# A spectral filter and a gated MLP on one core: the forward token transform in fp32 instead of three fp16 products

## The chip, the core and the metric

The kernel runs on one core of a Trainium2 chip. A core has a matrix engine (TensorE, PE in the profile; its weight loads are PEld), VectorE (DVE), ScalarE (ACT), GpSimd (POOL) and SyncE (SP), which here issues the DMAs. Each engine executes its own list of instructions in order and waits at semaphores for the others. SBUF holds operands; PE writes its sums to PSUM, from which ACT and DVE read them. The metric is the device time of one execution in microseconds (us), lower is better.

## The reference

The input `x` is 2048 tokens by 448 features, fp32. It is normalized over the features, and the normalized `xn` goes two ways:

```python
X = rfft2(xn)                       # over tokens and features
A = irfft2(X * (w_r + 1j * w_i))    # a filter in the frequency domain
gate = xn @ W_gate                  # 448 -> 1792
up   = xn @ W_up
h = gate * (gate > 0) * up
B = h @ W_down                      # 1792 -> 448
return x + A + B
```

## The kernel before

Both ways run at once. The matrix products of the MLP (gate and up, called `gu`, and down, `dn`) are the steady stream of PE. The Fourier transforms are cut into many small steps, mostly on DVE, that are strewn between them as background.

Precision is kept by splitting: a fp32 number is held as a high and a low fp16 half, and a product is three fp16 matmuls, high by high, high by low and low by high. Weights are split as they arrive (ACT makes the high half, DVE the low one, L924 and L928; for the down weights L957 and L961), and so is the activation `h` (L1028 to L1040: Relu on ACT, times up on DVE, high half on ACT, low half on DVE).

The two-dimensional transform is built in stages. The 2048 tokens are 16 residues by 128. The feature transform (`f_dft`, fp16 halves, 48 small matmuls of 58 columns) is done for two residues `a` and `a + 8` at a time. `f_fold` (L515) reads its PSUM and makes `Fq[a]`, the tile `eo` of the profile, fp32, of which there are two buffers. `f_a` and `f_b` (L444 to L467) take an eight-point transform over feature groups in place, on DVE. Then comes the token transform over 64 points, `f_sdft`, which this change touches. `f_hi` (ACT, L531) and `f_lo` (DVE, L534) split `eo` into the two fp16 halves `Xh`, for each of the two residues. `f_sdft` multiplies them by the table `fm`, in the four 64x64 quadrants of the array: quadrant (k, b) takes the rows of half k and writes the columns of half b. Its three products times four quadrants are 12 matmuls of 464 columns, and there are eight `f_sdft`, for a = 0, 4, 2, 6, 1, 5, 3, 7. Its result lies in the PSUM tile `fx`, of which there is one buffer of two banks, and `f_y1` reads it: ACT copies residue a to SBUF (L591), and DVE forms sum and difference with residue a + 8 (L596, L597). Further butterflies over the residues (`join2`, `join3`, L568 to L584), the filter product (L665 to L671), the inverse stages, the inverse token transform (`i_sdft`, `fx<-im,vt`) and the inverse feature transform (`i_ddft`, `fx<-idc_t,wf`) follow. The inverse stages need the butterflies of all sixteen residues.

The order of the work is set in three ways. The opening, to about 45 us, is written out by hand. After it the program walks through the MLP units, and hands out background items between them by credit: each item has a cost on DVE in microseconds (the number in `add`), and a factor `load` is found so that the costs of all items fill the room beside the units up to a place near the end. Then a list scheduler places the instructions on each engine by dependences and priorities. So a change to the items or their costs moves the background against the MLP everywhere after the opening. Gate and up sums use two PSUM tiles (`gu`) in turn: PE can start a unit only when DVE has read the one before the last (L1032).

Of the kernel before, what the change touches and what calls it, by code (L numbers as in the profile page):

```python
# [9 lines left out]
F16 = mybir.dt.float16  # L10
# [12 lines left out]
XW = NG * GW  # L23
# [77 lines left out]
def _constants():  # L101
# [17 lines left out]

    n1 = np.arange(64)  # L120
    k1, sine = _k1()
    c_fm = np.zeros((8, 2, 64, 2, 2, 64), np.float16)
    c_im = np.zeros((8, 128, 2, 2, 64), np.float16)
    for n2 in range(16):
        th = 2 * np.pi * (np.outer(16 * n1 + n2, k1) % S) / S
        w = np.where(sine[None, :], np.sin(th), np.cos(th))
        w[:, ROW] = (-1.0) ** n1
        c_fm[n2 % 8, n2 // 8] = np.stack(_split(w * sc), axis=1).reshape(64, 2, 2, 64).transpose(0, 2, 1, 3)
        c_im[n2 % 8, :, n2 // 8] = np.stack(_split(w.T * sc), axis=1)


# [18 lines left out]
    for s in range(8):  # L150
        th = 2 * np.pi * (np.outer(kp, m + s) % D) / D
        o = slice(56 * (s // 2), 56 * (s // 2) + 56)
        for c, t in enumerate((g * np.cos(th) * 8 / 7, -g * np.sin(th) * 8 / 7)):
            p = 64 * (s % 2) + 32 * c
            c_id[p:p + KC, :, o] = np.stack(_split(t), axis=1)
    c_fm = c_fm.reshape(2, 4, 128, 2, 2, 64).transpose(1, 2, 0, 3, 4, 5)
# [6 lines left out]
def tile_gfnet_reglu(ctx: ExitStack, tc: tile.TileContext, x, xr, wgu, wd, wf, ident, c_fd, c_fm, c_im, c_row, c_id,  # L163
# [70 lines left out]
    def ft(shape, dt, name, bufs=1):  # L234
        return fwd_pool.tile(shape, dt, name=name, bufs=bufs)
# [40 lines left out]
        nc.sync.dma_start(wdst[f], wdv[f])  # L276

    def load_fm(q):
        t = ft([128, 2, 2, 2, 64], F16, "fm", 4)
        nc.sync.dma_start(t, c_fm[q])  # L280
        for j in range(2):
            fm_t[q + 4 * j] = t[:, j]
# [253 lines left out]
    def f_sdft(a):  # L536
        m, w, ps = None, fm_t[a], fx2()
        for k in range(2):
            yps[a + 8 * k] = ps[:, k, 0:XW].rearrange("p (g c k) -> p g c k", g=NG, c=2)
        for i, (x, y) in enumerate(((0, 0), (0, 1), (1, 0))):  # L540
            for k in range(2):
                for b in range(2):
                    p, q = slice(64 * k, 64 * k + 64), slice(64 * b, 64 * b + 64)
                    xh = Xh[a + 8 * b].rearrange("p a g k -> p a (g k)")
                    with tc.high_priority(offset=0 if m is None else 2000):
                        m = chained(mm(ps[q, k, 0:XW], w[p, b, x], xh[p, y], start=(i == 0), stop=(i == 2),
                                       skip_group_check=True).ins, m)
        return m

    def rotate(t, b, p, sgn):  # L550
# [601 lines left out]
    for k, a in enumerate(seq):  # L1152
        gap = k and extra.get(k - 1)
        for second in (False, True):
            if second:
                add(1.99, f_a, a)
            if k and second != bool(gap):
                for n2 in (seq[k - 1], seq[k - 1] + 8):
                    add(1.09 * (n2 >= 8), f_y1, n2)
            if k < 7 and second != bool(gap):  # L1160
                add(0.0, offer, f_dft, seq[k + 1], seq[k + 1] + 8)
        add(2.14, f_b, a)
        for n2 in (a, a + 8):
            add(0.0, f_hi, a, n2)
        if k < 7:
            add(0.0, force, f_dft, seq[k + 1], seq[k + 1] + 8)
            add(1.27, f_fold, seq[k + 1])
        for n2 in (a, a + 8):
            add(0.54, f_lo, a, n2)
        add(0.0, f_sdft, a)  # L1170
        for fn, q in extra.get(k, ()):
            fn(q)
# [379 lines left out]
```

## Time and profile before

| | |
|---|---|
| time, median of 3 runs (lowest to highest) | 454.19 us (453.86 to 454.76) |
| the profiled execution: its time, its span | 452.46 us, 450.7 us |
| PE busy | 427.8 us, 95% of the span |
| DVE busy | 394.4 us, 88% |
| ACT busy | 252.8 us, 56% |
| mean granted PE clock | 0.985 |

The span goes from the first to the last instruction of the profiled execution. The page gives for each group of instructions its line, engine, operation, tiles (output<-inputs), count, busy time and mean duration, and behind the bar the idle time of the engine just before them with what ended it. Successive instructions of an engine overlap, so that the distance from start to start is less than the duration: a matmul of 512 columns lasts 380 ns by its group's mean, and twelve of `gu` take 2.70 us in the chain of waits. The page in forty slices:

```profile
PE   6999999999999999999999999979999973999997
DVE  6898898997987998999999999999998989958513
```

### The profile page before, as it was taken

The numbers are of one execution on the slowest core, as the hardware profiler recorded it, in microseconds if no ns is written. First come the engines' busy times: TensorE is split into PE (matmuls) and PEld (weight loads), VectorE is DVE, ScalarE is ACT, GpSimd is POOL, SyncE is SP. The second block draws the span as 40 slices with busy tenths as digits, with TensorE's granted clock in tenths as the row PEclk, the third lists the DMA queues.
The fourth block names the chain that finished last, engine by engine and source line by source line (L and its number), as shares of the span: only waits on it lengthen the run. The fifth ranks groups of instructions, "written<-read, shape, count | busy, mean of one in ns | idle before, by whom it ended". The sixth has DMA issues, their size and how long they took to land.

```text
span 450.7 us, 8697 instructions
## 1 busy us (share of the span) xinstructions
PE 427.8 (95%) x3254; PEld 203.4 (45%) x3254; DVE 394.4 (88%) x952; ACT 252.8 (56%) x508; POOL 32.2 (7%) x72
## 2 busy tenths in 40 slices
PE   6999999999999999999999999979999973999997
PEld 2644544444444444444444444434545432444544
DVE  6898898997987998999999999999998989958513
ACT  6897392387359746615434553935675663563630
POOL 1140030031001401000000010010000000000000
PEclk9999999999999999999999999999999995999999
DMA  8769948015002235334330310022122112300212
GB/s 263 243 165 291 373 118 123 2 36 72 3 2 93 67 117 155 81 89 123 87 84 1 100 27 1 1 55 53 29 50 70 37 35 51 105 22 1 83 42 81
DMA packets 37722, 38.63 MB, mean 86 GB/s; under 512 B 18928, under 2 KB 33072, under 8 KB 37680
## 3 DMA queue, kind: packets, MB, share of 16 engines
q1 hardware_dynamic: 37680, 38.09, 30.8%
q8 instruction: 25, 0.41, 0.4%
q14 instruction: 17, 0.14, 0.1%
HBM read 23.20 MB, written 3.67 MB: 60 GB/s over the span
## 4 chain that ended last, share of the span: by engine, by line
PE 51%; DVE 38%; ACT 6%; issue 2%; DMA 2%; SPq 0%; DVEq 0%; ACTq 0%
PE gu L476 31%; PE dn L476 13%; PE fx L476 4%; DVE h L1040 3%; DVE g L1032 3%; DVE y L568 2%; DVE y L569 2%; DVE wt L928 2%; ACT junk L219 2%; DVE y L665 2%; DVE y L668 2%; DVE y L583 2%; DVE y L706 1%; DVE y L584 1%; DVE y L707 1%
## 5 line engine op out<-in xcount | busy, mean ns | idle before, releaser
L476 PE MATMUL gu<-T,wt 128*128 128x512 f16 (+2 forms) x1250 | 270.9, 377 | 4.5 <-DVE g L1032 4.5
L476 PEld LDWEIGHTS <-wt 128*128 128x128 f16 (+1 forms) x1250 | 111.4, 98 | 148.3 <-issue 29.1
L476 PE MATMUL dn<-wdt,h 128*128 128x448 f16 x624 | 127.5, 353 | 0.0
L476 PEld LDWEIGHTS <-h 128*128 128x128 f16 x624 | 60.2, 98 | 57.9 <-issue 0.8
L1036 ACT ACTIVATE h<-g 128x512 f16<-128x512 f32 x56 | 35.1, 627 | 76.7 <-DVE g L1032 76.6
L1032 DVE SCALAR_TENSOR_TENSOR g<-gu,g 128x512 f32<-128x512 f32 x56 | 38.2, 683 | 14.3 <-ACT g L1028 14.2
L1040 DVE TENSOR_TENSOR h<-g,h 128x512 f16<-128x512 f32 x56 | 38.3, 685 | 10.0 <-ACT h L1036 9.9
L1028 ACT ACTIVATE g<-gu 128x512 f32<-128x512 f32 x56 | 32.8, 585 | 17.7 <-PE gu L476 17.7
L1068 ACT ACTIVATE xy<-dn,dsc 128x448 f32<-128x448 f32 x44 | 27.3, 624 | 12.8 <-PE dn L476 12.8
L1057 ACT ACTIVATE dn<-xy,dinv 128x448 f32<-128x448 f32 x44 | 27.5, 631 | 0.5
L928 DVE SCALAR_TENSOR_TENSOR wt<-wst,wsc,wt 128x512 f16<-128x512 f32 x28 | 20.3, 742 | 2.6 <-ACT wt L924 2.6
L222 POOL PARTITION_ALL_REDUCE wm<-wm x15 | 9.0, 598 | 161.0 <-ACT junk L219 161.0
L924 ACT ACTIVATE wt<-wst,wsc 128x512 f16<-128x512 f32 x28 | 19.1, 713 | 1.8 <-DVE wsc L229 1.8
L219 ACT ACTIVATE junk<-wst 128x512 bf16<-128x512 f32 x28 | 17.4, 620 | 1.3 <-DMA wst<-in_wgu 1.1
L810 ACT ACTIVATE vt<-wst,fsc 128x928 f16<-128x928 f32 x8 | 8.8, 1099 | 10.8 <-DVE wst L467 10.8
L957 ACT ACTIVATE wdt<-wdst,wds 128x448 f16<-128x448 f32 x14 | 8.7, 658 | 8.5 <-DVE wds L953 8.5
L569 DVE TENSOR_TENSOR y<-y,y 128x464 f32<-128x464 f32 x21 | 13.3, 633 | 0.1
L568 DVE TENSOR_TENSOR y<-y,y 128x464 f32<-128x464 f32 x21 | 13.3, 632 | 0.1
L657 ACT ACTIVATE wf<-wf 128x116 f32<-128x116 f32 x16 | 4.5, 293 | 15.8 <-DMA wf<-in_wf 15.8
L839 DVE SCALAR_TENSOR_TENSOR yu<-fx,yu 128x512 f32<-128x512 f32 x16 | 11.0, 687 | 2.6 <-ACT yu L834 2.3
L860 ACT ACTIVATE fx<-xy,fsc 128x448 f32<-128x448 f32 x14 | 8.8, 629 | 7.9 <-DVE yu L839 7.9
L291 DVE BATCH_NORM_STATS2 bst<-y 128x6 f32<-128x448 f32 x16 | 9.2, 617 | 4.3 <-DMA y<-in_xr 4.3
(164 smaller groups left out, 506.2 us busy)
## 6 DMA issues: line engine op xcount, KB each, us to landing
wst<-in_wgu SPq DMA_DIRECT2D x28, 256.0 KB, 4.7
wf<-in_wf SPq DMA_DIRECT2D x16, 232.0 KB, 2.8
sw<-y SPq DMA_DIRECT2D x64, 58.0 KB, 2.0
sw<-wst SPq DMA_DIRECT2D x32, 116.0 KB, 2.2
y<-in_xr SPq DMA_DIRECT2D x16, 224.0 KB, 4.9
xy<-in_x SPq DMA_DIRECT2D x16, 224.0 KB, 5.0
out<-xy SPq DMA_DIRECT2D x15, 224.0 KB, 1.9
wdst<-in_wd SPq DMA_DIRECT2D x14, 224.0 KB, 4.6
```

Source lines behind the costliest of these rows:

```text
L219: A.activation(mt([128, 512], BF16, "junk")[:, 0:src.shape[-1]], src, AF.Square, scale=SQ, accum_out=acc)
L476: r = P.matmul(*a, **k)
L568: V.tensor_tensor(t, a, b, op=OP.add)
L569: V.tensor_tensor(d, a, b, op=OP.subtract)
L924: A.activation(w[:, 0:4, :], wst[f, g], AF.Copy, scale=wsc[f, g])
L928: V.scalar_tensor_tensor(w[:, 4:8, :], st, sc, w[:, 0:4, :], op0=OP.mult, op1=OP.subtract)
L1028: last["A"] = A.activation(g1s[f, q], hps[f, q][:, 0, :], AF.Relu, scale=2.0 ** -22).ins
L1032: last["V"] = V.scalar_tensor_tensor(g1, hps[f, q][:, 1, :], 2.0 ** -22, g1, op0=OP.mult, op1=OP.mult).ins
L1036: A.activation(ht[f, q][:, 0, :], g1s[f, q], AF.Copy)
L1040: V.tensor_tensor(h[:, 1, :], g1s.pop((f, q)), h[:, 0, :], op=OP.subtract)
L1057: A.activation(dps[n2][:, 0:D], xy[n2], AF.Copy, scale=dinv[:, g:g + 1])
L1068: last["A"] = A.activation(xy[n2], dps[n2][:, 0:D], AF.Copy, scale=dsc[:, g:g + 1]).ins
```

## The change

The split before the token transform is left out. `f_hi` and `f_lo` are no longer called, and `f_sdft` multiplies the fp32 part of `Fq[a]` (`f_part`, a strided view of `eo`) by an fp32 table, one matmul for each quadrant instead of three. The table holds the unsplit numbers, at the same size in bytes. The items of `f_hi` and `f_lo`, the latter at 0.54 us each, leave the list of the background, by which `load` and all that follows is set. The functions `f_hi` and `f_lo` stay in the text but are not used.

```diff
-    c_fm = np.zeros((8, 2, 64, 2, 2, 64), np.float16)
+    c_fm = np.zeros((8, 2, 64, 2, 64), np.float32)
...
-        c_fm[n2 % 8, n2 // 8] = np.stack(_split(w * sc), axis=1).reshape(64, 2, 2, 64).transpose(0, 2, 1, 3)
+        c_fm[n2 % 8, n2 // 8] = (w * sc).reshape(64, 2, 64)
...
     def load_fm(q):
-        t = ft([128, 2, 2, 2, 64], F16, "fm", 4)
+        t = ft([128, 2, 2, 64], F32, "fm", 4)
...
     def f_sdft(a):
         m, w, ps = None, fm_t[a], fx2()
...
-        for i, (x, y) in enumerate(((0, 0), (0, 1), (1, 0))):
-            for k in range(2):
-                for b in range(2):
-                    p, q = slice(64 * k, 64 * k + 64), slice(64 * b, 64 * b + 64)
-                    xh = Xh[a + 8 * b].rearrange("p a g k -> p a (g k)")
-                    with tc.high_priority(offset=0 if m is None else 2000):
-                        m = chained(mm(ps[q, k, 0:XW], w[p, b, x], xh[p, y], start=(i == 0), stop=(i == 2),
-                                       skip_group_check=True).ins, m)
+        for k in range(2):
+            for b in range(2):
+                p, q = slice(64 * k, 64 * k + 64), slice(64 * b, 64 * b + 64)
+                with tc.high_priority(offset=0 if m is None else 2000):
+                    m = chained(mm(ps[q, k, 0:XW], w[p, b], f_part(a, a + 8 * b)[p], start=True, stop=True,
+                                   skip_group_check=True).ins, m)
...
         add(2.14, f_b, a)
-        for n2 in (a, a + 8):
-            add(0.0, f_hi, a, n2)
         if k < 7:
             add(0.0, force, f_dft, seq[k + 1], seq[k + 1] + 8)
             add(1.27, f_fold, seq[k + 1])
-        for n2 in (a, a + 8):
-            add(0.54, f_lo, a, n2)
         add(0.0, f_sdft, a)
```

Line numbers behind the touched functions are smaller by 2 in the changed kernel (L596 becomes L594, L1032 becomes L1030), and by 6 at its end.

How instructions stand on PE at the seventh token transform, before (buffer numbers kept; the two `Xh` are the two residues):

```order
L476 MATMUL dn_2383<-wdt_604,h_2158 128x448
L476 LDWEIGHTS fm_1301
L476 MATMUL fx_2006<-Xh_1946,fm_1301 64x464
L476 LDWEIGHTS fm_1301
L476 MATMUL fx_2006<-Xh_1948,fm_1301 64x464
```

and now:

```order
L476 LDWEIGHTS h_1794
L476 MATMUL dn_2327<-wdt_601,h_1794 128x448
L476 MATMUL fx_1898<-eo_1775,fm_1269 64x464 x4
L476 LDWEIGHTS h_1794
L476 MATMUL dn_2327<-wdt_601,h_1794 128x448
```

Twelve pairs of a weight load and a matmul have become four matmuls without a weight load between them, on the fp32 tiles.

On DVE, the end of the forward part, before. L466 and L467 end the last eight-point transform, L596 and L597 are the butterflies that read a token transform's PSUM (the second pair those of the last one), L1032 and L1040 the gate product and the low half of `h`:

```order
L467 SCALAR_TENSOR_TENSOR eo<-bw 128x2x116
L961 SCALAR_TENSOR_TENSOR wdt<-wdst,wds,wdt 128x448
L596 TENSOR_TENSOR y_81<-y_73,fx 128x464
L597 TENSOR_TENSOR y_69<-y_73,fx 128x464
L1032 SCALAR_TENSOR_TENSOR g_2335<-gu,g_2335 128x512
L534 TENSOR_TENSOR Xh<-eo,Xh 128x464 x2
L1040 TENSOR_TENSOR h<-g_2335,h 128x512
L1032 SCALAR_TENSOR_TENSOR g_2377<-gu,g_2377 128x512
L1040 TENSOR_TENSOR h<-g_2377,h 128x512
L596 TENSOR_TENSOR y_78<-y_75,fx 128x464
L597 TENSOR_TENSOR y_77<-y_75,fx 128x464
```

and now:

```order
L467 SCALAR_TENSOR_TENSOR eo<-bw 128x2x116
L951 TENSOR_SCALAR wds<-wds 128x5
L959 SCALAR_TENSOR_TENSOR wdt<-wdst,wds,wdt 128x448 x2
L1030 SCALAR_TENSOR_TENSOR g_2266<-gu,g_2266 128x512
L1038 TENSOR_TENSOR h<-g_2266,h 128x512
L594 TENSOR_TENSOR y_78<-y_75,fx 128x464
L595 TENSOR_TENSOR y_77<-y_75,fx 128x464
L566 TENSOR_TENSOR y_73<-y_81,y_78 128x464
L567 TENSOR_TENSOR y_75<-y_81,y_78 128x464
L1030 SCALAR_TENSOR_TENSOR g_2321<-gu,g_2321 128x512
```

The two subtractions of the split are gone, one gate product stands behind the last butterflies of the forward part instead of ahead of them, and the butterflies of the seventh transform have moved further ahead.

The gate product that follows next on DVE, before:

```order
L583 SCALAR_TENSOR_TENSOR y_69<-y_79,y_67 128x464
L584 SCALAR_TENSOR_TENSOR y_75<-y_79,y_67 128x464
L961 SCALAR_TENSOR_TENSOR wdt<-wdst,wds,wdt 128x448
L568 TENSOR_TENSOR y_67<-y_72,y_78 128x464
L569 TENSOR_TENSOR y_79<-y_72,y_78 128x464
L1032 SCALAR_TENSOR_TENSOR g_2592<-gu,g_2592 128x512
L575 TENSOR_TENSOR y_72<-y_82,y_77 128x8x29
```

and now:

```order
L581 SCALAR_TENSOR_TENSOR y_69<-y_79,y_67 128x464
L582 SCALAR_TENSOR_TENSOR y_75<-y_79,y_67 128x464
L1030 SCALAR_TENSOR_TENSOR g_2502<-gu,g_2502 128x512
L566 TENSOR_TENSOR y_67<-y_72,y_78 128x464
L567 TENSOR_TENSOR y_79<-y_72,y_78 128x464
L731 SCALAR_TENSOR_TENSOR rowh<-row,rowh 16x232
```

The product stands ahead of the butterfly (L568 and L569, now L566 and L567) that preceded it. Two weight splits further up and the one shown (L961, now L959) stand behind it as well.

More of the change, by code (lines that the diff above doesn't have):

```diff
@@ L155, in _constants @@
             c_id[p:p + KC, :, o] = np.stack(_split(t), axis=1)
-    c_fm = c_fm.reshape(2, 4, 128, 2, 2, 64).transpose(1, 2, 0, 3, 4, 5)
+    c_fm = c_fm.reshape(2, 4, 128, 2, 64).transpose(1, 2, 0, 3, 4)
     ident = np.eye(128, dtype=np.float16)
```

## The prediction

> **What bounds the kernel now.** I read the page's engine rows first, then the same engines stretch by stretch, since two engines near full load can take turns as the bound.
>
> ```profile
> PE 427.8 (95%) x3254; PEld 203.4 (45%) x3254; DVE 394.4 (88%) x952; ACT 252.8 (56%) x508; POOL 32.2 (7%) x72
> ...
> 45.00:170.00 125.00, 123.91 (x1024) 56.76 (x1022) 114.42 (x297) 74.15 (x154) 16.50 (x30) 1.00 0.36 91
> 172.00:313.00 141.00, 137.59 (x678) 62.68 (x677) 138.82 (x327) 69.02 (x158) 4.58 (x6) 1.00 0.25 65
> 313.00:363.00 50.00, 50.00 (x554) 24.89 (x553) 45.34 (x99) 33.08 (x54) 0.00 (x0) 1.00 0.22 53
> 363.00:382.00 19.00, 8.78 (x168) 5.38 (x166) 18.42 (x43) 8.97 (x15) 0.00 (x0) 0.69 0.15 34
> 382.00:450.70 68.70, 65.39 (x596) 33.00 (x594) 39.65 (x83) 30.13 (x48) 0.00 (x0) 0.99 0.16 55
> ```
>
> In the rows by stretch come start and end, length, then PE, PEld, DVE, ACT and POOL busy, and the granted clock. The forward transform runs at 45 to 170 us: PE is busy for 123.91 of 125 us, DVE for 114.42. So there PE is the bound and DVE has 10.6 us to spare. From 172 to 313 both are full. From 363 to 382 PE stands for 10.2 us while DVE works: PE has reached a place in its order where the inverse transform must be ready, and DVE, late by then, makes it wait. The clock granted there falls to 0.69. After 382 PE is the bound again, to the end. A change pays at the end if DVE reaches that place earlier, and costs if DVE or PE reaches it later.
>
> Who waits for whom says how close the two engines run in the middle:
>
> ```profile
> PE gu L476 <- DVE g L1032: 4.5, 3, 2.8
> ...
> 154.80 0.38 PE L476 MATMUL gu<-T,wt 128*128 128x512 f16 x1 [1.09 <-DVE g L1032]
> ```
>
> PE waits three times, 4.5 us in all, for DVE to empty a gate/up accumulator (the product at L1032); the first, 1.09 us, lies in the forward stretch. Elsewhere there PE runs without a pause.
>
> **The change, part by part.**
>
> *DVE and ACT lose the split.* Both halves of it, and the tail of the forward stretch on DVE:
>
> ```profile
> L534 DVE TENSOR_TENSOR Xh<-eo,Xh 128x464 f16<-128x464 f32 x16 | 9.7, 635 | 1.8 <-ACT Xh L531 1.8
> L531 ACT ACTIVATE Xh<-eo 128x464 f16<-128x464 f32 x16 | 8.9, 595 | 4.4 <-DVE eo L467 4.3
> ...
> 167.78 1.18 DVE L534 TENSOR_TENSOR Xh<-eo,Xh 128x464 f16<-128x464 f32 x2
> 168.88 0.68 DVE L1040 TENSOR_TENSOR h<-g,h 128x512 f16<-128x512 f32 x1
> ...
> 171.86 0.64 DVE L596 TENSOR_TENSOR y<-y,fx 128x464 f32<-128x464 f32 x1 [0.31 <-ACT y L591]
> ```
>
> Sixteen subtractions of 635 ns go, but they overlap at their ends: two take 168.88 - 167.78 = 1.10 us from start to the next start. So DVE gains 8 x 1.10 = 8.8 us of room, and 1.8 us in which it waited for ACT. ACT gains 8.9 us busy; at 56% it binds nowhere for long. All of this lies before 170 us, where DVE already has 10.6 us idle, so by itself it is worth nothing to the end. It pays only if what follows on DVE can start earlier, and that is the question of the next part.
>
> *PE: ninety-six fp16 matmuls become thirty-two in fp32.* One transform now, looked at in three narrow windows, and in the chain of waits:
>
> ```profile
> 110.14 0.39 PE L476 MATMUL fx<-Xh,fm 64*64 64x464 f16 x4
> 110.14 0.59 PE L476 MATMUL fx<-Xh,fm 64*64 64x464 f16 x8
> 110.14 0.78 PE L476 MATMUL fx<-Xh,fm 64*64 64x464 f16 x12
> ...
> 62.31 0.71 PE fx L476 x12
> 63.02 2.70 PE gu L476 x12
> ...
> L476 PEld LDWEIGHTS <-fm 64*64 64x64 f16 x96 | 2.2, 105 | 4.4 <-issue 3.0 <-DVE eo L457 0.4 <-DVE eo L461 0.4
> ```
>
> Four matmuls, one in each 64x64 quadrant of the array, run side by side: 0.39 us for four, 0.59 for eight, 0.78 for twelve. A round of four costs 0.195 us and a transform three rounds; to the next gate/up matmul it takes 0.71 us.
>
> No fp32 matmul is in this trace, so its price must be bounded. The kernel's own split says what full precision takes: an fp32 number is held as a high and a low half, and three of the four products of halves are computed. A full fp32 product has all four, so I count four passes of 0.195 us for each of the four matmuls of a transform, sixteen in all. The ends are then set by how they overlap. Below: all quadrants side by side, as now, 4 rounds, 0.78 us, 0.195 more than today. Lower still, below nothing: two passes side by side, 0.39 us, a gain of 0.195. Above: nothing overlaps, 16 x 0.195 = 3.12 us, 2.54 more. I take a value between, from the order. Before, successive matmuls go to different quadrants, and that is why four run together. Now one quadrant's passes are one row of the program, all four behind each other, and only where one quadrant ends and the next begins can they meet. If half of a matmul's passes (those with one half of the weights) meet half of its neighbour's, five pairs stand in a row: 10 x 0.195 = 1.95 us, 1.37 more than 0.585. Eight transforms: 8 x 1.37 = 11.0 us on PE, in the stretch where PE is full.
>
> The Trainium skill speaks to both points. FP8 and Floating Point Precision, section TensorE Precision Notes, says that true fp32 takes four passes through the array, which is the sixteen. TensorE: Matmul & The Clock Gate, section Part 3, says that matmuls start and end strictly in program order, so a second pass held up in its own quadrant holds up the other quadrants behind it; this speaks against the change, since without that rule the sum would be the 4 rounds. The trace agrees as far as it goes: rounds begin 0.195 us apart and none overtakes.
>
> The weights of the fp16 matmuls were loaded by separate instructions (105 ns each), ahead. The new order shows none: an fp32 matmul loads its own. If nothing hides one load in each matmul, 32 x 0.105 = 3.4 us come on top; I leave that to the range. The table's DMAs (`fm<-in_c_fm`) keep their bytes, two fp16 halves against one fp32.
>
> *What moves.* Counted in the order, the eighth and last transform stood behind 514 gate/up and 220 down matmuls and now stands behind 508 and 206. These rows price it:
>
> ```profile
> 45.72 2.65 PE dn L476 x14
> ...
> 168.09 0.39 PE L476 MATMUL fx<-Xh,fm 64*64 64x464 f16 x4
> ...
> 181.44 0.39 PE L476 MATMUL gu<-T,wt 64*128 64x512 f16 x2
> ...
> 171.35 0.48 ACT y L591
> ...
> 183.63 0.68 DVE L961 SCALAR_TENSOR_TENSOR wdt<-wdst,wds,wdt 128x448 f16<-128x448 f32 x1
> 184.22 0.63 DVE L568 TENSOR_TENSOR y<-y,y 128x464 f32<-128x464 f32 x1
> 184.78 0.63 DVE L569 TENSOR_TENSOR y<-y,y 128x464 f32<-128x464 f32 x1
> 185.33 0.68 DVE L1032 SCALAR_TENSOR_TENSOR g<-gu,g 128x512 f32<-128x512 f32 x1
> ...
> 361.73 0.60 ACT L1028 ACTIVATE g<-gu 128x512 f32<-128x512 f32 x1 [0.47 <-PE gu L476]
> 362.36 0.69 DVE L1032 SCALAR_TENSOR_TENSOR g<-gu,g 128x512 f32<-128x512 f32 x1 [0.38 <-ACT g L1028]
> ```
>
> 14 down matmuls take 2.65 us and 6 gate/up ones 6 x 2.70/12 = 1.35: 4.0 us earlier. Against it stand seven longer transforms, 7 x 1.37 = 9.6 us, and the wait of 1.1 at 154.80 goes because DVE is no longer late. The last transform then starts at 168.1 - 4.0 - 1.1 + 9.6 = 172.6 and, at 0.71 + 1.37, ends at 174.7; ACT's copy (L591, 0.48 us) makes it 175.2. L596, the butterfly that reads it, ran at 171.86. It had waited only 0.31 us, so DVE and PE met there; now PE is the later, by 3.3 us, and DVE's 8.8 us are spent waiting ahead of it. *That is where the saving goes.*
>
> Next in DVE's order is the gate product that ran at 185.33. Its accumulator was closed by the half passes from 181.44 on, the last of four ending near 182.05. Moved by 11.0 - 1.1 it is full at 191.95, and the shortest path to the product (Relu at 361.73, product at 362.36) adds 0.63: 192.6, or 7.3 us later than before. In the new order this product also stands ahead of three weight splits and one butterfly that came before it: 3 x 0.59 + 2 x 0.55 = 2.9 us that DVE now has behind it (L961 starts 0.59 before the next row, L568 and L569 some 0.55). From there to 382 DVE is the full engine, so the join comes 7.3 + 2.9 = 10.2 us later by this route and 3.3 by the other. DVE was idle for 2.2 us at 172 to 313 and 4.7 at 313 to 363, waits that a late DVE does not have in full; I let a quarter of that, 1.7, absorb it.
>
> **Sum:** 8.5 us later at the join, and all after it unchanged. The profiled execution took 452.46 us (span 450.7), so 461.0; it lies 1.73 under the median of the runs, 454.19, on which the forecast stands: 454.2 + 8.5 = **462.7 us**.
>
> Edits at nothing: the fp32 operand is the eight-point result itself, which stays in use until the matmul instead of until the subtraction; the fold that writes its buffer next (L515, two transforms on, at 73.37 after a transform at 62.31) comes some 10 us later:
>
> ```profile
> 73.37 1.19 DVE L515 SCALAR_TENSOR_TENSOR eo<-fx,y 128x464 f32<-128x464 f32 x2 [0.94 <-ACT y L504]
> ```
>
> Without that cover DVE would wait for one transform, 2 us.
>
> **Rivals**, each by the same route (moved PE end, plus 2.9, less 1.7).
>
> - *Nothing overlaps.* The wider operand, or its own weight loads, keep the quadrants apart: 16 passes, 8 x 2.54 = 20.3 us. 182.05 + 20.3 - 1.1 + 0.63 - 185.33 = 16.5; join 17.7 later: 471.9 us. For it: one instruction a quadrant, no load ahead. Against: the quadrants are independent in every row now.
> - *Side by side after all.* 4 rounds, 8 x 0.195 = 1.6 us: -2.2 at the product, join 1.0 earlier: 453.2 us, no change to speak of. Against it stands that each quadrant's passes follow each other.
> - *Faster.* Fp32 goes at half rate instead of a quarter, two passes, four quadrants side by side: 0.39 us, PE gains 8 x 0.195 = 1.6. Then the product is ready 5.4 us earlier, the join 4.1: 450.1 us. By this route the join moves by eight times the added cost less 2.55 us, so a transform must cost under 0.71 + 2.55/8 = 1.0 us; above that PE takes back what DVE saved. The Trainium skill, Perfetto Trace Analysis, section Engine Utilization, halves the peak for a mode it calls FP32_LOW_HIGH, which would give this; no row here shows that mode.
> - That the change does not do what it says is excluded by the order: no Xh, no weight load, one row of fp32 operands.
>
> **How the numbers follow.** Forecast 0.50, nothing overlaps 0.24, side by side 0.12, half rate 0.14. The likeliest alone spans 459 to 466 (the 3.3 us route to the 3.4 us of loads, roughly). For 8 times in 10 the range must take in side by side below and most of the serial case above: 452 to 473. A measurement of this kernel tells 0.2%, 0.9 us, from no change: the half-rate case and some of the side-by-side one give faster 0.16, most of the rest of that one same 0.08, slower 0.76.
>
> **What would show it.** In the changed profile the fx matmuls from eo should take about 2.1 us from their first start to the next gate/up matmul (0.7 or less: faster; 3.2 or more: nothing overlaps). DVE should stand idle by some 20 us at 45 to 175, with waits for PE ahead of L594 (the old L596) and of the gate product after it. PE should stand for about 10 us near 370 to 390, as now. I am wrong if that last gap is gone, since then DVE's saving got through, or if PE stands idle in the forward stretch, since then it was not the bound.

## The result, and the profile after

The changed kernel took 449.69 us (median of 4 runs, 448.99 to 450.31), the kernel before 454.48 us on the same chip: ratio 0.9892, 95% interval 0.9869 to 0.9916. It became 1.1% faster. The forecast was 462.7 us, slower, and the time lies below its range. The profiled execution took 449.81 us, span 448.0 us, mean granted PE clock 0.984.

The engine row of the page and the windows by stretch, in the same columns as before (start and end, length, then PE, PEld, DVE, ACT and POOL busy, then the granted clock):

```profile
PE 430.8 (96%) x3222; PEld 203.1 (45%) x3222; DVE 386.0 (86%) x936; ACT 246.3 (55%) x492; POOL 29.6 (7%) x72
```

```profile
45.00:170.00 125.00, 125.00 (x992) 56.44 (x991) 108.55 (x287) 67.86 (x140) 14.30 (x38) 1.00 0.33 96
172.00:313.00 141.00, 139.47 (x729) 63.45 (x728) 138.30 (x322) 69.30 (x155) 5.43 (x6) 1.00 0.23 62
...
363.00:382.00 19.00, 10.64 (x170) 5.86 (x168) 18.69 (x47) 9.01 (x14) 0.00 (x0) 0.65 0.20 55
```

PE has 3.0 us more to do (430.8 for 427.8), and the span is 2.7 us shorter all the same, so PE stands idle for 5.7 us less. In the forward stretch, 45 to 170 us, it is full; DVE's work there fell from 114.42 to 108.55 us. At 172 to 313 PE's idle time went from 3.4 to 1.5 us, at 363 to 382 from 10.2 to 8.4 us.

One token transform, in PE's timeline (start, duration, group, count):

```profile
78.09 1.03 PE L476 MATMUL fx<-eo,fm 64*64 64x464 f32 x8
79.06 0.39 PE L476 MATMUL gu<-T,wt 128*128 128x512 f16 x1
```

It takes 79.06 - 78.09 = 0.97 us to the next gate/up matmul, where the split took 0.71. Eight matmuls, not four: each fp32 matmul is two passes. In a narrower window, up to 78.3 us, four of them have started:

```profile
78.09 0.63 PE L476 MATMUL fx<-eo,fm 64*64 64x464 f32 x4
```

So the first passes of the four quadrants run side by side, and then the second ones. All eight transforms take 0.966 us to the next matmul, rounded to thousandths; before, seven took 0.714 (in the eighth, down matmuls stand between). That is 0.25 us more each, 8 x 0.25 = 2.0 us.

The end of the forward part on DVE, the last butterflies of the token transforms (L594) and the gate product that the prediction followed (L1030 at 178.73):

```profile
166.88 0.63 DVE L594 TENSOR_TENSOR y<-y,fx 128x464 f32<-128x464 f32 x1
...
178.73 0.68 DVE L1030 SCALAR_TENSOR_TENSOR g<-gu,g 128x512 f32<-128x512 f32 x1
```

The first is 5.0 us earlier than before (171.86), the second 6.6 (185.33). And the waits of PE at the join, before and after, in PE's timeline (in brackets the idle time before a row and what ended it; `im` is the inverse token transform, `idc_t` the inverse feature transform):

```profile
367.35 0.23 PE L476 MATMUL fx<-idc_t,wf 64*128 64x56 f16 x4
367.81 1.03 PE L476 MATMUL fx<-idc_t,wf 64*128 64x56 f16 x44 [0.23 <-DVE wf L849]
372.52 0.29 PE L476 MATMUL fx<-im,vt 64*128 64x64 f16 x4 [3.68 <-ACT vt L810]
374.45 1.36 PE L476 MATMUL fx<-im,vt 64*128 64x64 f16 x44 [1.65 <-DVE vt L815]
380.18 0.28 PE L476 MATMUL fx<-idc_t,wf 64*128 64x56 f16 x4 [4.37 <-ACT fx L860]
```

```profile
365.36 0.79 PE L476 MATMUL fx<-idc_t,wf 64*128 64x56 f16 x48
365.99 0.59 PE L476 MATMUL gu<-T,wt 64*128 64x512 f16 x4
369.45 1.65 PE L476 MATMUL fx<-im,vt 64*128 64x64 f16 x48 [2.87 <-ACT xy L874]
376.40 0.28 PE L476 MATMUL fx<-idc_t,wf 64*128 64x56 f16 x4 [5.30 <-ACT fx L858]
```

Before, three inverse pieces stand in PE's order with no MLP matmul between them: idct, im, idct. Each needs what DVE and ACT make of the one ahead, so PE waits for each in turn. Now four gate/up matmuls stand between the first two. Pieces with no MLP matmul between them are said below to stand in a row; this row turned out to be what most of the experiments are about.

### The profile page after: what moved, and what is told of

Read it like the earlier page. It is cut to its first block, busy times and chain, and to the rows that moved or that the text cites. A ratio compares the mean times of both kernels' runs of the same rounds, so it can differ in the third digit from the quotient of the medians.

```text
span 448.0 us, 8595 instructions
## 1 busy us (share of the span) xinstructions
PE 430.8 (96%) x3222; PEld 203.1 (45%) x3222; DVE 386.0 (86%) x936; ACT 246.3 (55%) x492; POOL 29.6 (7%) x72
## 4 chain that ended last, share of the span: by engine, by line
PE 49%; DVE 32%; ACT 7%; DMA 5%; SPq 3%; issue 2%; POOL 0%; DVEq 0%; ACTq 0%
PE gu L476 30%; PE dn L476 12%; PE fx L476 4%; DVE h L1038 3%; DVE g L1030 3%; DMA sw<-y 3%; SPq L696 2%; DVE y L567 1%; DMA wf<-in_wf 1%; DVE y L566 1%; DVE yu L837 1%; DVE y L663 1%; DVE wf L847 1%; DVE y L666 1%; DVE y L581 1%
## 5 line engine op out<-in xcount | busy, mean ns | idle before, releaser
L1030 DVE SCALAR_TENSOR_TENSOR g<-gu,g 128x512 f32<-128x512 f32 x56 | 38.3, 683 | 16.7 <-ACT g L1026 16.6
L222 POOL PARTITION_ALL_REDUCE wm<-wm x15 | 10.6, 708 | 171.2 <-ACT junk L219 171.2
L515 DVE SCALAR_TENSOR_TENSOR eo<-fx,y 128x464 f32<-128x464 f32 x16 | 9.5, 634 | 9.3 <-ACT y L504 9.3
L566 DVE TENSOR_TENSOR y<-y,y 128x464 f32<-128x464 f32 x21 | 13.3, 634 | 0.4 <-DMA row<-y 0.3
L567 DVE TENSOR_TENSOR y<-y,y 128x464 f32<-128x464 f32 x21 | 13.3, 634 | 0.1
L476 PE MATMUL fx<-idc_t,wf 64*128 64x56 f16 x384 | 7.2, 189 | 5.5 <-ACT fx L858 5.3
L813 DVE SCALAR_TENSOR_TENSOR vt<-wst,fsc,vt 128x464 f16<-128x464 f32 x16 | 10.5, 698 | 2.3 <-ACT vt L808 2.3
```

Source lines behind the costliest of these rows:

```text
L476: r = P.matmul(*a, **k)
L566: V.tensor_tensor(t, a, b, op=OP.add)
L567: V.tensor_tensor(d, a, b, op=OP.subtract)
L1030: last["V"] = V.scalar_tensor_tensor(g1, hps[f, q][:, 1, :], 2.0 ** -22, g1, op0=OP.mult, op1=OP.mult).ins
```

## Experiments

### The fp32 matmul by itself

The whole computation is left out. After a warm-up PE repeats: the twelve fp16 matmuls of a transform (`tst_half`), its four fp32 matmuls in the four quadrants (`tst_four`), and four fp32 matmuls all in one quadrant, in two quadrants that share rows, in two that share columns, and on the full 128x128 array (`tst`), with fp16 matmuls (`warm`) between.

```diff
+    pats = {
+        "half": ([(k, b) for _ in range(3) for k in range(2) for b in range(2)], w16, m16),
+        "four": ([(k, b) for k in range(2) for b in range(2)], w32, m32),
+        "one": ([(0, 0)] * 4, w32, m32),
+        "rows": ([(0, 0), (0, 1)] * 2, w32, m32),
+        "cols": ([(0, 0), (1, 0)] * 2, w32, m32),
+    }
```

> Measures the price of fp32 matmuls alone; the whole computation is left out (the input is copied to the output). Tiles of 64x64, 464 columns, each pattern four times after a warm-up: twelve fp16 over four quadrants (as before the change), four fp32 over four quadrants (as now), four fp32 all in one quadrant, four over two quadrants that share rows, four over two that share columns, and four full 128x128 fp32. Theory A (each quadrant has its own line, a held-up pass holds up only its own quadrant): a fp32 matmul is two passes of about 0.45 us; four quadrants 0.9 us per transform, one quadrant 8 x 0.39 to 0.46 = 3.1 to 3.7 us, two quadrants half of that, 1.6 to 1.8 us. Theory B (the prediction's: matmuls start strictly in program order): four quadrants about 1.9 us, one quadrant 3.1, two quadrants 1.9 to 2.3.

PE's timeline, one repetition of each. Of the rows named `tst`, the one at 37.30 is one quadrant, 55.44 two quadrants that share rows, 79.23 the full array (two quadrants that share columns read 67.38 and 69.09, as far apart as the two that share rows):

```profile
20.44 0.78 PE L186 MATMUL tst_half<-m,w 64*64 64x464 f16 x12
21.16 0.96 PE L193 MATMUL warm<-m,w 128*128 128x464 f16 x4
...
28.41 1.01 PE L186 MATMUL tst_four<-m,w 64*64 64x464 f32 x8
29.36 0.96 PE L193 MATMUL warm<-m,w 128*128 128x464 f16 x4
...
37.30 3.32 PE L186 MATMUL tst<-m,w 64*64 64x464 f32 x8
40.55 0.96 PE L193 MATMUL warm<-m,w 128*128 128x464 f16 x4
...
55.44 1.77 PE L186 MATMUL tst<-m,w 64*64 64x464 f32 x8
57.15 0.96 PE L193 MATMUL warm<-m,w 128*128 128x464 f16 x4
...
79.23 3.28 PE L213 MATMUL tst<-m,w 128*128 128x464 f32 x8
82.34 1.73 PE L193 MATMUL warm<-m,w 128*128 128x464 f16 x8
```

From start to the next start: 0.72 us for the fp16 twelve, 0.95 for four fp32 matmuls in four quadrants, 3.25 in one, 1.71 in two whether they share rows or columns. So the quadrants do not hold each other up: the eight passes take 3.25/8 = 0.41 us each in a row, and in four quadrants two rounds of 0.475, in which the start and the end weigh more. From the first pass of a quadrant to its second it takes 0.44 us in both patterns. The price of the change on PE is 0.95 - 0.72 = 0.23 us a transform, as in the kernel (0.25). The prediction's 1.37 is out.

### Parts of the change, one at a time

Five kernels put one part back or take one part alone. All experiments with times ran on several chips, on which the kernel before, run beside them, read 453.58 to 455.11 us; a difference of about 1 us between two of them is to be read from the ratios. In `e1_split_kept` the fp32 transform is there, and the split is still computed, with nobody reading it:

```diff
         add(2.14, f_b, a)
+        for n2 in (a, a + 8):
+            add(0.0, f_hi, a, n2)
...
+        for n2 in (a, a + 8):
+            add(0.54, f_lo, a, n2)
         add(0.0, f_sdft, a)
```

> The changed kernel, with the split into two fp16 halves still computed on ACT and DVE at its old place and cost, but read by nobody. If the time was won by the room on DVE and ACT, it is lost again and PE's longer transforms (8 x 0.25 = 2.0 us) remain: 454.5 + 2.0 = 456.5 us. If it was won by the shorter path (the transform no longer waits for two splitting steps), it stays near 449.7 us.

Measured 457.69 us, ratio 1.0073 (1.0048 to 1.0099). With the split kept, the fp32 transforms cost 3.6 us over before, as the first of the two theories had it; with the split's work and its cost back in, the gain is gone.

`e2_no_low_half` keeps fp16 and leaves out the low halves of `Xh`: their product reads the high half instead, so the output lacks them, and PE has the same work as before.

```diff
-                        m = chained(mm(ps[q, k, 0:XW], w[p, b, x], xh[p, y], start=(i == 0), stop=(i == 2),
+                        m = chained(mm(ps[q, k, 0:XW], w[p, b, x], xh[p, 0], start=(i == 0), stop=(i == 2),
...
-        for n2 in (a, a + 8):
-            add(0.54, f_lo, a, n2)
```

> The kernel before with the low half of the operand left out: DVE's sixteen subtractions and their cost in the list are gone, ACT's high half stays, and the second product reads the high half again, so PE does the same twelve fp16 matmuls (the result lacks the low halves). If DVE's room is what counts, all of the change's gain without PE's 2.0 us: 449.7 - 2.0 = 447.7 us. If ACT's room or the shorter path is needed as well, less: 450 to 453 us.

Measured 452.8 us, ratio 0.9973 (0.9958 to 0.9989): 1.3 us, which is the second of the two expected outcomes and much less than the first. Its order has the three inverse pieces in a row, as before.

`e3_twice` does each fp32 transform twice, which is 1.77 us for 0.97 in its trace, 8 x 0.80 = 6.4 us more on PE:

```diff
-        for k in range(2):
-            for b in range(2):
+        for k, b in [(k, b) for _ in range(2) for k in range(2) for b in range(2)]:
+            if True:
```

> The changed kernel with each fp32 token transform made twice, one after the other: 8 x 0.91 = 7.3 us more on PE in the forward stretch, nothing else. If PE bounds that stretch and nothing behind takes it up (the prediction's premise), 449.7 + 7.3 = 457.0 us. If the join behind has room, under 453 us.

Measured 456.4 us, ratio 1.0057 (1.0028 to 1.0086): 6.7 us over the changed kernel, 7.5 by the ratios, with the pieces of the join behind the same numbers of MLP matmuls. PE's work in the forward stretch counts about one for one, as the prediction had it.

Then the split's parts put back into the changed kernel. `e6_act_half_kept`: ACT's half. `e7_dve_half_kept`: sixteen DVE subtractions of the same size, at the old place and cost, result unused.

```diff
+        for n2 in (a, a + 8):
+            add(0.0, f_hi, a, n2)
```

> The changed kernel with only ACT's high half still computed and read by nobody (8.9 us busy on ACT, none on DVE). Keeping both halves cost 8.0 us (457.7 against 449.7), and taking DVE's half alone out of the kernel before brought 1.3. If ACT's half carries what is left, about 455 us; if the two must go together, 450 to 452.

```diff
     def f_lo(a, n2):
-        V.tensor_tensor(Xh[n2][:, 1], f_part(a, n2), Xh[n2][:, 0], op=OP.subtract)
+        Xh[n2] = ft([128, 2, 2 * NG, KC], F16, "Xh", 2)
+        V.tensor_tensor(Xh[n2][:, 1], f_part(a, n2), f_part(a, n2), op=OP.subtract)
...
+        for n2 in (a, a + 8):
+            add(0.54, f_lo, a, n2)
```

> The changed kernel with only sixteen subtractions on DVE kept at their place and cost in the list, each of the operand from itself, so that they wait for no ACT and nobody reads them (8.8 us on DVE). If DVE's room is what counts, nearly all of the 8.0 us: 456 to 458. If it is ACT's half or the path through both, 450 to 452.

`e6` took 452.63 us (0.9982, 0.9962 to 1.0003), `e7` 457.42 (1.0104, 1.007 to 1.0137): 2.9 and 7.7 us over the changed kernel. ACT's half binds nowhere and still costs 2.9; in its order, though, the three pieces stand in a row again. That was the first sign that an edit's work is not all that is measured here.

### The list: costs and factor

The costs of the background list set the planner's factor `load` (in the expectations also the pace): it came out as 1.000 in before and 0.974 in the changed kernel, since 16 x 0.54 us left the list. `e4_costs_kept` is the changed kernel with sixteen empty items of that cost, `e5_costs_out` the kernel before with the cost of `f_lo` set to nothing.

```diff
+        for n2 in (a, a + 8):
+            add(0.54, lambda: None)
```

> The changed kernel, with sixteen empty items of cost 0.54 us where the low halves stood in the list: same work as the changed kernel, but the background is handed out at the pace of the kernel before (the eighth transform stands behind 511 gate/up and 215 down matmuls instead of 508 and 206). If the work removed is what pays, it stays at 449.7 us within 1. If the faster pace is what pays, most of the gain goes: 452 to 455 us.

```diff
-            add(0.54, f_lo, a, n2)
+            add(0.0, f_lo, a, n2)
```

> The kernel before with the cost of the low halves set to 0 in the list: same work as before, handed out at the pace of the changed kernel. If pace alone pays, 450 to 452 us. If the work removed pays, 454.1 us within 1, or slower, since DVE is asked for more than it has.

`e4` took 453.41 us (0.9991, 0.9971 to 1.0011), `e5` 454.51 (1.0016, 1.0001 to 1.0032). So the whole edit of the computation, with the list as it was, is worth nothing that can be measured, and 3.7 us, by the ratios 1.0% of the changed kernel's 1.1%, come with the list. I took this for a theory of pace: a list with true costs lets the work come earlier, and pays where DVE has room. It was put to the test by scaling the factor.

```diff
-    load[0] = hi
+    load[0] = 0.97 * hi
```

The other three have 1.03 and 1.06 in the changed kernel, and 1.06 in the kernel before.

> The changed kernel with one number changed: the planner's factor, with which the background's costs are spread over the MLP's, is 0.97 of the value it found, so background pieces follow each other 3% more slowly in TensorE's order. Pace theory (a list with the eviction's and the forward transforms' true costs lets the same work come earlier, and where VectorE has room the earlier order is worth 3.7 us): a slower pace gives back part of it, 451 to 454 us. Rival (the 3.7 us is the accident of one scheduler's order, in which one piece fewer stands at the join): any time between 449 and 455 with no regular move along 0.97, 1, 1.03, 1.06.

> The changed kernel with the planner's factor at 1.03 of the value it found. Pace theory: the forward stretch goes on earlier by some 3% of 172 us if VectorE keeps up, and the wait of TensorE at the join (8.35 us in the changed kernel) gets shorter: 446 to 449 us, if the inverse transforms' pieces do not stop at another place. Rival (accident of the order): 449 to 455, no order with 0.97 and 1.06.

> The changed kernel with the planner's factor at 1.06 of the value it found; the order's background then ends before the MLP's last units, so fewer pieces stand alone behind the join. Pace theory: 443 to 448 us as long as VectorE's room (16.5 us idle in the forward stretch) covers the faster pace; where it does not, TensorE waits at the evictions and the time is back at 450 or above. Rival (accident of the order): within 2 to 3 us of 450, either side.

> The kernel before with the planner's factor at 1.06 of the value it found, and nothing else. Pace theory with room: VectorE has 10.6 us idle in its forward stretch against 16.5 us, and a quicker list alone gave nothing (454.51), so 453 to 457 us. Rival (the planner's factor is simply too low, for any split): as much gain as at 1.06 in the changed kernel, 447 to 450 us.

443.77 us (ratio 0.9782, 0.9747 to 0.9817) at 0.97, 451.9 at 1.03 (0.998, 0.9961 to 1.0), 467.39 at 1.06 (1.0316, 1.0284 to 1.0348), and 458.42 for before at 1.06 (1.0107, 1.0066 to 1.0149). The theory falls, with its sign: the slower list is the faster kernel, and the step to 0.97 moves the time by more than the change did. The rival on record, times from 449 to 455 with no order in them, holds at 1.03 alone. PE's timeline of the slowest, 467.39 us, shows why:

```profile
311.86 0.29 PE L476 MATMUL fx<-im,vt 64*128 64x64 f16 x4 [3.34 <-ACT vt L808]
...
320.85 0.28 PE L476 MATMUL fx<-idc_t,wf 64*128 64x56 f16 x4 [6.30 <-ACT fx L858]
...
325.43 0.29 PE L476 MATMUL fx<-im,vt 64*128 64x64 f16 x4 [2.87 <-ACT vt L808]
...
332.49 0.28 PE L476 MATMUL fx<-idc_t,wf 64*128 64x56 f16 x4 [4.38 <-ACT fx L858]
```

Four inverse pieces stand in a row. From the start of one piece to the start of the next it takes 4.6 to 9.0 us, and with no MLP matmul between, PE stands for most of it while DVE and ACT work.

The kernel before then got lower factors too, 0.974 and 0.945 of its own (whose value is 1.000), and the changed kernel 0.94 and 0.91 of its 0.974; the edit is the same line.

> The kernel before with the planner's factor at 0.974 instead of 1.000: the factor that the changed kernel has. Theory R (the split's room on VectorE is what pays, and the factor only places it): the work that is left at equal factor is 8.8 us more on VectorE, so 451 to 454 us, against 449.7 of the changed kernel. Theory F (the factor pays, whatever the split): 448 to 450 us, no slower than the changed kernel at this factor, so the change itself would be worth nothing.

> The kernel before with the planner's factor at 0.945. The changed kernel took 443.8 us there. Theory R: VectorE is 4 to 5 us later at the join as in every pair so far, TensorE's pieces wait for it, 447 to 451 us. Theory F: the lower factor places the inverse pieces so late that VectorE is in time either way, and TensorE has 3.0 us less work with the fp16 products: 441 to 444 us.

> The changed kernel with the planner's factor at 0.916 (0.94 of its own). Both theories: TensorE's waits before 382 us are nearly gone (5.4 us were left at 0.945, of them 4.0 near 369), and what is left of the inverse stages behind the last MLP unit grows by a piece or two of some 1 us. 442 to 446 us; a time above 447 would mean that the gain at 0.945 was the accident of one order.

> The changed kernel with the planner's factor at 0.886 (0.91 of its own). In its order five inverse feature transforms stand behind the last MLP matmuls on TensorE, against one or two at 0.945, so the end is set by VectorE and ScalarE alone: 446 to 455 us if a piece that stands bare costs 1 to 3 us. If the time stays at 442 to 444, the end has room for them.

The kernel *before* took 439.51 us at 0.974 (0.9689, 0.9656 to 0.9721), faster than the changed kernel at any factor tried so far, and 450.7 at 0.945 (0.9929, 0.9905 to 0.9954). The changed kernel took 450.22 at 0.916 (0.9912, 0.9882 to 0.9943) and 456.76 at 0.886 (1.0072, 1.0046 to 1.0099). Theory R had the second right and missed the first by 11 us: before is at its best with all the split's work in it. Theory F missed both: there is no smooth best factor. The two of the changed kernel also lie above what was expected, 442 to 446 and 446 to 455. What goes with the time is the order. For each kernel, how many MLP matmuls stand on PE between one inverse piece and the next where they stand closest, and the sum of PE's waits of over 0.05 us from 45 us on:

| kernel | time, us | closest inverse pieces on PE (MLP matmuls between in brackets) | PE's waits, us |
|---|---|---|---|
| before, 0.974 (`e12`) | 439.51 | no two closer than 17 | 3.8 |
| changed, 0.945 (`e8`) | 443.77 | im [6] id | 5.4 |
| changed, 0.974 | 449.69 | id [4] im [0] id | 9.9 |
| changed, 0.916 (`e14`) | 450.22 | im [8] id, and im [0] id at the end | 10.0 |
| before, 0.945 (`e13`) | 450.7 | im [8] id, and id [4] im near the end | 11.7 |
| changed, costs kept, 1.000 (`e4`) | 453.41 | id [0] im [0] id | 12.8 |
| before, 1.000 | 454.0 | id [0] im [0] id | 14.7 |
| changed, DVE half kept, 1.000 (`e7`) | 457.42 | id [0] im [0] id | 15.6 |
| changed, 1.033 (`e10`) | 467.39 | im [0] id [0] im [0] id | 26.5 |

The closer the pieces, the longer PE waits, and the time goes with the waits. The runs that the table leaves out fit in: 451.9 us with 11.7 us of waits (`e9`), 452.63 with 12.6 (`e6`), 452.8 with 14.0 (`e2`), 454.51 with 15.4 (`e5`), 457.69 with 15.5 (`e1`), 458.42 with 15.8 (`e11`), 456.76 with 16.4 (`e15`, with five pieces in a row behind the last MLP matmul); only `e3`, which has 6.4 us more of work, lies apart with 456.4 and 10.0. The factor by itself does not order them. `e2`, `e5` and `e6` have the changed kernel's 0.974, and all three have three pieces in a row, like before. `e5` and `e12` are even the same work at the same factor, with the cost of `f_lo` out of the list or in it, and they take 454.51 and 439.51 us.

### The change at equal order

The last two runs test this. `e16_after_costs_kept_0974` is `e4` with the factor 0.974 of `e12`: from the third inverse piece on, its pieces stand behind the same numbers of MLP matmuls as in `e12`. `e17_after_factor_096` is the changed kernel with its own list at 0.985 of its factor, an order without a row.

```diff
+        for n2 in (a, a + 8):
+            add(0.54, lambda: None)
...
-    load[0] = hi
+    load[0] = 0.974 * hi
```

> The changed kernel with the old costs kept in the list (sixteen empty items of 0.54 us) and the factor at 0.974: from the fifth inverse piece on, every inverse transform stands behind the same number of gate/up and down matmuls as in the kernel before at 0.974, which took 439.5 us, and no two stand in a row. Order theory (the time is set by which inverse pieces stand in a row; the change is worth next to nothing at equal order, as in the two pairs with like orders so far, 454.1 against 453.4 and 450.7 against 450.2): 438.5 to 441 us. Theory P (TensorE is full, so its longer transforms count): 441.5 to 443. Theory R (VectorE's 8.8 us of room count): 434 to 437.

```diff
-    load[0] = hi
+    load[0] = 0.985 * hi
```

> The changed kernel with its own list and the factor at 0.985 of its own, 0.960: between 0.974 (449.7 us, two pieces in a row behind gate/up matmul 1110) and 0.945 (443.8). In its order no two inverse transforms stand in a row up to the end. Order theory: the join's 8.35 us of waiting nearly go, 439 to 443 us. Rival (the factor itself, not the row): half way between its neighbours, 446 to 447.

`e16` took 440.29 us (0.9684, 0.9658 to 0.971), against `e12`'s ratio of 0.9689: no difference. Order theory has it. `e17` took 438.89 us (0.9655, 0.9631 to 0.9679), just under its range for the order theory, 2.4% less than the changed kernel and the fastest of all, though by ratio not apart from `e12`. Windows of `e12`, then of `e17`:

```profile
45.00:170.00 125.00, 124.86 (x1033) 57.63 (x1032) 116.42 (x300) 75.87 (x157) 14.11 (x38) 1.00 0.34 94
...
363.00:382.00 19.00, 18.65 (x180) 9.24 (x179) 17.36 (x42) 12.29 (x19) 0.00 (x0) 1.00 0.20 55
```

```profile
45.00:170.00 125.00, 125.00 (x993) 56.49 (x992) 108.29 (x286) 67.08 (x139) 14.27 (x38) 1.00 0.33 97
...
363.00:382.00 19.00, 19.00 (x184) 9.48 (x182) 17.19 (x40) 11.91 (x20) 0.00 (x0) 1.00 0.18 47
```

DVE has 8 us more to do in the first at 45 to 170, and both have lost the join: PE is busy for 18.65 and 19.00 of the 19 us at 363 to 382, and its clock no longer falls there (1.00 for 0.65). That is part of the price of a row. The changed kernel and `e17` have the same matmuls, and their spans differ by 448.0 - 437.4 = 10.6 us: 9.9 - 2.5 = 7.4 are PE's waits, and 430.8 - 427.4 = 3.4 are busy time, in the trace whose clock falls. The timeline of `e17` around the same place:

```profile
359.42 6.00 PE L476 MATMUL gu<-T,wt 128*128 128x512 f16 x27
365.26 2.06 PE L476 MATMUL dn<-wdt,h 128*128 128x448 f16 x10
367.25 0.60 PE L476 MATMUL gu<-T,wt 64*128 64x512 f16 x3
367.48 0.94 PE L476 MATMUL fx<-idc_t,wf 64*128 64x56 f16 x46
...
368.56 4.49 PE L476 MATMUL gu<-T,wt 128*128 128x512 f16 x20
372.89 1.30 PE L476 MATMUL dn<-wdt,h 128*128 128x448 f16 x6
374.12 0.87 PE L476 MATMUL fx<-im,vt 64*128 64x64 f16 x48
```

Ahead of the idct piece stand 40 MLP matmuls, some 8 us, and behind it 26, some 6 us; DVE and ACT are done in time.

Three pairs have like orders of the inverse pieces on both sides: before and `e4`, 454.0 and 453.4 us on one chip; `e13` and `e14`, much alike up to the last third of the pieces, 450.7 and 450.2; `e12` and `e16`, ratios 0.9689 and 0.9684. In none can a difference be measured; the intervals of these ratios reach 0.2 to 0.3% either way, so that an effect of 1 us, or a little more, would not show. In the first pair one can see what cancels: `e4` has 12.8 us of PE's waits for 14.7 in before, and its transforms take 2.0 us more. So the change by itself is worth nothing that can be measured here, and the 1.1% goes with the order that it made.

## Why the prediction was wrong

The forecast lies 462.7 - 449.7 = 13.0 us too high. The price of the transform is 11.0 - 2.0 = 9.0 of it; nearly all of the rest is the order at the join, of which the list alone brings 3.7 us (`e4` against the changed kernel).

**The price of the fp32 transform.** The step "five pairs stand in a row: 10 x 0.195 = 1.95 us, 1.37 more than 0.585" failed in the overlap. The passes of the four quadrants run side by side, all of them, so that no quadrant is held up by another. They are also two passes a matmul and not four, but each as long as two of mine. Measured: 0.966 us to the next matmul where the split took 0.714, so 0.25 more, 2.0 us in all where I had 11.0. The rivals at 4 rounds (0.195 more) and at half rate (0.39 us, a gain) each had one part of it: four quadrants side by side, and two passes, but a pass of 464 columns takes as long as two of fp16 (0.41 us for 0.195). The first of them, at a chance of 0.12, comes within 0.06 us of the measured price. TensorE: Matmul & The Clock Gate of the Trainium skill, section Part 3, which I had weighed against the change, says that matmuls start in strict program order. The trace shows the four first passes and then the four second ones, but not in which order the program names the eight, so it neither agrees nor disagrees; that a quadrant's two passes stand behind each other there was my assumption, and four quadrants in 0.95 us against one in 3.25 rule out what I built on it. The Trainium skill's FP8 and Floating Point Precision, section TensorE Precision Notes, names four passes for fp32; as sixteen rounds of 0.195 us they would fill 3.12 us in one quadrant, and 3.25 was measured there, so the amount holds where its packing did not.

**"DVE's 8.8 us are spent waiting ahead of it."** That rested on the 11.0. The step itself was sound: with 0.25 for 1.37 it puts the last transform at 168.1 - 4.0 - 1.1 + 7 x 0.25 = 164.75, and it began at 164.56. So PE was not 3.3 us late at L594, and the butterfly ran 5.0 us earlier. With the old list, putting DVE's work back costs 457.42 - 453.41 = 4.0 us in fp32 (`e7` and `e4`, which both have three pieces in a row). With fp16 products the pair is `e5` and `e2`: every inverse piece stands behind the same numbers of MLP matmuls in both, neither has the cost in its list, and `e2` alone lacks DVE's half: 454.51 and 452.8 us, by ratio 0.43% or 2.0 us, with intervals that do not overlap. So the sentence "by itself it is worth nothing to the end" was wrong, although DVE had 10.6 us of idle time in that stretch. What the work costs shows in PE's waits for the gate product. They are in `e7`, then in `e4` (in all, how often, the longest):

```profile
PE gu L476 <- DVE g L1031: 4.4, 4, 2.6
```

```profile
PE gu L476 <- DVE g L1030: 2.4, 1, 2.4
```

`e5` has 4.5 us of them and `e2` 3.1. The added ones lie mostly between 222 and 265 us, in the stretch in which DVE is full: there it is still behind with what it did not get done. What else is in the 4.0 us between `e7` and `e4`, whose orders differ by a few matmuls, stays open.

**The gate product, "192.6, or 7.3 us later".** It ran at 178.73, 13.9 us ahead of that. The transforms' price explains 9.0 of it. The rest is a position: I left its accumulator at its old place on PE, and took from the order only the six gate/up and fourteen down matmuls that the *transform* had passed. PE's timelines, before and after, from the last transform to the accumulator's close (some 12 of the 33 in the last row before, the end of the last row after; before, three more down matmuls stand between the matmuls of the transform):

```profile
170.02 1.50 PE L476 MATMUL dn<-wdt,h 128*128 128x448 f16 x7
171.35 0.81 PE L476 MATMUL gu<-T,wt 128*128 128x512 f16 x3
172.00 3.00 PE L476 MATMUL dn<-wdt,h 128*128 128x448 f16 x15
174.84 1.89 PE L476 MATMUL gu<-T,wt 128*128 128x512 f16 x8
176.56 3.00 PE L476 MATMUL dn<-wdt,h 128*128 128x448 f16 x15
179.40 7.07 PE L476 MATMUL gu<-T,wt 128*128 128x512 f16 x33
```

```profile
164.56 1.03 PE L476 MATMUL fx<-eo,fm 64*64 64x464 f32 x8
165.53 1.47 PE L476 MATMUL gu<-T,wt 128*128 128x512 f16 x6
166.83 4.70 PE L476 MATMUL dn<-wdt,h 128*128 128x448 f16 x24
171.37 5.02 PE L476 MATMUL gu<-T,wt 128*128 128x512 f16 x24
```

Counted over the whole traces, the accumulator closes behind 538 gate/up matmuls in both, but behind 260 down matmuls before and 230 after. These 30 are 30 x 2.65/14 = 5.7 us. So the accumulator was full near 176.4 us, 15.6 earlier than the 191.95 of the prediction, of which 9.0 + 5.7 = 14.7 are accounted for; the product then came 2.3 us behind it and not 0.63, as DVE had other work until then. The 30 could be counted in the order ahead of the run, as the twenty were.

**The join, "8.5 us later ... and all after it unchanged".** The end of the join's last wait came at 376.40 us, 3.8 earlier than 380.18. Its price is also not fixed, and this is the larger fault. I took the gap of 10.2 us as a place at which DVE is late, while it is the number of inverse pieces that stand in a row: with none, it is 0 to 0.4 us in the same stretch (`e17`, `e12`). I counted positions where the changed lines are, at the eighth transform, and not at the place which I had named as deciding the end.

**What held.** PE is the bound of the forward stretch: full for 125.00 of 125 us, and an added microsecond there costs about one (`e3`, 6.7 for 6.4). The rule that "a transform must cost under 0.71 + 2.55/8 = 1.0 us" to be faster has the right side at 0.97. Put in as 0.25, it gives the join 0.55 us earlier and 453.7 us; with the old list `e4` took 453.41. The agreement is of little weight, since the product step in it is wrong for the changed kernel. Of my two signs of error, the gap's vanishing and an idle PE in the forward stretch, neither came: the gap of 10.2 us is 8.4. The transform's time, read first, did tell.

**The account of the gain.** From before (454.11 us beside `e1`) to `e1` +3.6 us (fp32 on PE, split kept), to `e7` -0.3 (ACT's half gone), to `e4` -4.0 (DVE's half gone), to the changed kernel -3.7 (costs out of the list, two pieces in a row instead of three), together -4.4. By the ratios the steps are +0.7, +0.3, -1.1 and -1.0%, so that the one for ACT's half cannot be told from none. The first three terms, in kernels with the same three pieces in a row, cancel; the last one is an order that another factor improves by some ten more. In the traces of `e4` and the changed kernel the last step is 452.1 - 448.0 = 4.1 us of span, of which 12.8 - 9.9 = 2.9 are waits of PE and 432.0 - 430.8 = 1.2 are busy time. What stays open is why the scheduler puts three pieces at one spot, in seven of the kernels behind 1110 gate/up and 548 down matmuls; no run took the scheduler apart.

## What to carry to other kernels

Where a planner spreads background work over a full engine, any edit of its list is two changes, the work and the order, and the second can be the larger one: measure the edit at equal order too, here by keeping the costs in the list or by moving its factor on both sides. Before forecasting, count in the order of the full engine how much independent work stands between each two dependent pieces, at the place where the profile shows the wait and not only where the code changed. An fp32 matmul took about four times an fp16 one here, in one quadrant (0.81 us for 0.195) and in four side by side (0.95 for a third of 0.72); that the four still ran side by side is what made it cheaper than forecast. Measure the passes in a loop of their own first.

## What the runs showed of the hardware

- Each fp32 matmul shows in the trace as two weight loads and two matmuls: 64 of each for 32 in the program, though the order names no weight load. Loads of 64x64 weights took 131 ns in fp32, 105 in fp16.

```profile
L476 PE MATMUL fx<-eo,fm 64*64 64x464 f32 x64 | 8.3, 586 | 0.0
L476 PEld LDWEIGHTS fx<-eo,fm 64*64 64x64 f32 x64 | 1.7, 131 | 3.1 <-issue 1.1 <-ACT dn L1055 0.8 <-ACT xy L1066 0.4
```

- Four fp32 matmuls of 464 columns took 3.11 us on the full array (82.34 - 79.23), 0.78 each, and 3.25 us in one 64x64 quadrant: a smaller tile by itself saves nothing, two quadrants halve it (1.71), four bring 0.95.
- In the stretches shown above the granted clock was 1.00 where PE waited for 3.4 us or less of 125 to 141 us, and 0.65 to 0.69 in the 19 us that hold 8.4 to 10.2 us of the join's waits. Long waits of PE there come with a slower clock: `e17`, which has none, shows a mean of 0.999 for the changed kernel's 0.984.
